# Row-tiled pairs for the last 64 rows of D, a 512-column gate|up operand, a new ScalarE order and an even spread of gradient pieces

## Chip, cores, metric

One core of a Trainium2 chip. The metric is device microseconds (us) of one execution, median of several. Before: 1578.2 us (1576.9 to 1579.3, 4 runs).

## The reference

The kernel gives the output and seven gradients of a gated mix: a = a 2-D FFT filter of x, b = a GEGLU feed-forward of x; out = g a + (1 - g) b with g = sigmoid(sum of x * gate_w).

```python
B, S, D, F = 1, 2048, 576, 4608
g = _sigmoid((x * gate_w).sum(-1, keepdims=True))
a = _A_ref(x, A_w_r, A_w_i)              # irfft2(rfft2(x) * W)
b = (_gelu(x @ w_gate) * (x @ w_up)) @ w_down
return g * a + (1 - g) * b               # and its vjp for grad_out
```

D = 576 is four and a half times 128. That half is what the change is about.

## The kernel before

First stage: 18 groups of 256 hidden columns x 8 steps of two 128-row tiles of x, 144 "hidden steps". A step computes gate and up of x and dOT (the gradient times w_down transposed), then GELU and its derivative. PSUM is the memory that TensorE writes its results to, in banks; ScalarE or VectorE must copy a result out before its bank can be used again. Into the steps are mixed "transform units" of the FFT (two PSUM banks, one unit at a time; a step has two places for them, its "half steps") and "gradient pieces" of the weights (dwd, dw, tail; two PSUM banks). A second stage reads the hidden gradients back and makes the outputs.

```python
DCH = [(0, 128), (128, 128), (256, 128), (384, 128), (448, 128)]  # last chunk overlaps, half zeroed
ph = ...tile_pool(name="ph", bufs=4, space=PSUM)   # 4 x one bank: gate, up, dOT of a step and one more
pw = ...tile_pool(name="pw", bufs=2, space=PSUM)   # gradient pieces
pf = ...tile_pool(name="pf", bufs=1, space=PSUM)   # transform units, two banks

def H_mm(g, tp):                                   # line 312
    for w, xt in ((wg_g, xT), (wu_g, xT), (wdT_g, dOT)):
        pt = ph.tile([P, TPB, FG], F32, tag="hps", name="hps")
        for tt in range(TPB):
            for ci in range(5):
                nc.tensor.matmul(pt[:, tt, :], lhsT=xt[:, ci, tp * TPB + tt, :], rhs=w[:, ci, :],
                                 start=(ci == 0), stop=(ci == 4))
# (cut) ScalarE in H_ew1: q, xb (gate), hu (up), om, s (sigmoids), da (dOT)
for step ...:
    fft_until(want(step, 0)); pts = H_mm(g, tp)
    tiles = H_ew1(g, tp, pts); fft_until(want(step, 1)); H_ew2(g, tp, tiles)
    for _ in range(quota[tp]):                     # quota = [0, 1, 1, 1, 2, 1, 2, 1]
        if pend: pend.pop(0)()                     # gradient pieces of the last group
# (cut) second stage: six transposing loads, then wd_all (3 x 1.7 MB), then the last pieces
```

## Time and profile before

| | before |
|---|---|
| time | 1578.2 us |
| TensorE busy | 1510 us, 96% |
| waiting of TensorE, from its start distances | 81 us |
| of it in 0 to 150 us / 150 to 1150 / 1150 to 1250 | 42 / 27 / 12 |

TensorE's busy time overlaps from matmul to matmul. "Waiting" here is each start-to-start distance less the time the earlier matmul streams (columns / 2.4 + 2.5 ns, that is 109 for 256 columns and 123 for 288, the distances that the trace shows where nothing waits). A pair that starts together counts once. This is worked out from the trace's records. Where the clock is at half, as in parts of the start, the slower streaming is in it too. The busy time by stretch (columns: stretch, length, busy us and count of TensorE, weight loads, VectorE, ScalarE, GpSimd, granted clock, DMA share, GB/s), kernel before:

```profile
0.00:150.00 150.00, 118.21 (x1070) 98.40 (x1071) 97.90 (x284) 107.22 (x191) 8.49 (x25) 0.94 0.50 133
150.00:400.00 250.00, 242.17 (x2192) 207.99 (x2190) 153.09 (x419) 161.56 (x310) 0.00 (x0) 1.00 0.37 103
400.00:650.00 250.00, 241.97 (x2184) 208.21 (x2183) 202.74 (x526) 165.37 (x321) 0.00 (x0) 0.99 0.47 134
```

TensorE is nearly full from 150 us on.

### The profile page before, as it was taken

The page shows a single profiled execution, that of the slowest core. Times are in us where ns is not written, and L with a number is a line of the kernel's source. Part 1 is how long each engine was busy: PE and PEld are TensorE (multiplying, and loading weights), DVE is VectorE, ACT ScalarE, POOL GpSimd, SP SyncE. Part 2 cuts the span into 40 slices and gives each one's busy share as a digit, 9 for nine tenths or more (in the row PEclk, how much of TensorE's full clock was granted, in tenths as well). Part 3 has the DMA queues.
Part 4 walks back from the last instruction along what each step waited for, and adds up shares of the span by engine and source line. Part 5 has one row for each costly group of instructions (what it writes and reads, how often), then busy time and mean ns, then how long its engine had stood idle before and what let it go on. Part 6 is the DMA issues. An engine that isn't in the chain of part 4 may idle for free.

```text
span 1576.6 us, 33157 instructions
## 1 busy us (share of the span) xinstructions
PE 1510.1 (96%) x13310; PEld 1270.9 (81%) x13310; DVE 813.9 (52%) x2154; ACT 738.8 (47%) x1395; POOL 26.3 (2%) x58
## 2 busy tenths in 40 slices
PE   6798999999999999999999999999997999999998
PEld 4577888888788888888888888888876777777776
DVE  5775565666887877865555646667103212121210
ACT  6777665765766766665666656656000000000000
POOL 1000000000000000000000000000000000000000
PEclk8999999999999999999999999999999999999999
DMA  6632432334544544453424434364899978787873
GB/s 140 198 102 78 113 99 82 109 97 132 140 134 120 151 124 129 132 152 93 124 82 135 127 97 128 101 145 122 241 192 214 212 153 172 155 171 154 170 150 69
DMA packets 513435, 214.45 MB, mean 136 GB/s; under 512 B 318080, under 2 KB 506368, under 8 KB 513280
## 3 DMA queue, kind: packets, MB, share of 16 engines
q1 hardware_dynamic: 511648, 207.61, 54.5%
q0 software_dynamic: 1632, 4.72, 1.1%
q8 instruction: 104, 1.70, 0.5%
q14 instruction: 51, 0.42, 0.1%
HBM read 41.77 MB, written 94.71 MB: 87 GB/s over the span
## 4 chain that ended last, share of the span: by engine, by line
PE 62%; issue 23%; DVE 6%; ACT 6%; DMA 1%; POOL 1%; SPq 1%; POOLq 0%; DVEq 0%; ACTq 0%
PE hps L312 25%; PE wps L392 15%; PE wps L376 7%; PE pf L640 3%; PE acc L833 2%; PE wps L403 2%; PE pf L433 2%; PE acc L875 2%; ACT da L334 1%; ACT om L330 1%; ACT q L323 1%; DMA pin<-scr 1%; PE pf L624 1%; PE pf L626 1%; ACT xb L324 1%
## 5 line engine op out<-in xcount | busy, mean ns | idle before, releaser
L312 PEld LDWEIGHTS <-xT 128*128 128x128 bf16 x2880 | 286.0, 99 | 39.6
L875 PEld LDWEIGHTS <-pin 128*128 128x128 bf16 x2304 | 225.4, 98 | 58.3 <-DMA pin<-scr 1.6
L392 PEld LDWEIGHTS <-xn 128*128 128x128 bf16 x2304 | 223.9, 98 | 30.3 <-issue 3.6
L312 PE MATMUL hps<-wg_g,xT 128*128 128x256 bf16 x1440 | 186.5, 278 | 0.0
L312 PE MATMUL hps<-wu_g,xT 128*128 128x256 bf16 x1440 | 183.8, 275 | 0.0
L312 PE MATMUL hps<-wdT_g,dOT 128*128 128x256 bf16 x1440 | 180.8, 273 | 0.0
L325 DVE TENSOR_SCALAR s<-q 128x512 bf16<-128x512 bf16 x144 | 42.0, 291 | 254.0 <-ACT q L323 253.8
L312 PEld LDWEIGHTS <-dOT 128*128 128x128 bf16 x1440 | 141.0, 98 | 16.4
L833 PE MATMUL acc<-wd_all,pin 128*128 128x288 bf16 x1152 | 145.4, 288 | 8.1 <-DMA pin<-scr 6.6
L376 PE MATMUL wps<-dB,A 128*128 128x288 bf16 x1152 | 152.2, 286 | 0.0
L875 PE MATMUL acc<-wuT,pin 128*128 128x288 bf16 x1152 | 143.4, 286 | 1.3 <-DMA pin<-scr 1.3
L833 PEld LDWEIGHTS <-pin 128*128 128x128 bf16 x1152 | 113.2, 98 | 38.5 <-DMA pin<-scr 7.5
L875 PE MATMUL acc<-wgT,pin 128*128 128x288 bf16 x1152 | 143.4, 286 | 0.0
L376 PEld LDWEIGHTS <-A 128*128 128x128 bf16 x1152 | 112.7, 98 | 27.6
L392 PE MATMUL wps<-dHu,xn 128*128 128x256 bf16 x1152 | 131.7, 273 | 0.0
L392 PE MATMUL wps<-dHg,xn 128*128 128x256 bf16 x1152 | 131.5, 273 | 0.0
L323 ACT ACTIVATE q<-hps 128x512 bf16<-128x512 f32 x144 | 86.1, 598 | 94.9 <-PE hps L312 94.9
L885 ACT COPY f32t<-acc 128x576 f32<-128x576 f32 x16 | 10.2, 638 | 250.5 <-PE acc L875 250.5
L334 ACT ACTIVATE da<-hps,omg 128x256 bf16<-128x256 f32 x288 | 118.1, 460 | 0.0
L887 DVE SCALAR_TENSOR_TENSOR f32t<-gwf,dlog,f32t 128x576 f32<-128x576 f32 x16 | 13.1, 818 | 179.1 <-ACT f32t L885 179.1
L330 ACT ACTIVATE om<-s 128x512 bf16<-128x512 bf16 x144 | 91.0, 632 | 24.5 <-DVE s L326 23.9
L331 ACT ACTIVATE s<-s 128x512 bf16<-128x512 bf16 x144 | 90.7, 630 | 4.6
(164 smaller groups left out, 1760.9 us busy)
## 6 DMA issues: line engine op xcount, KB each, us to landing
scr<-A SPq DMA_DIRECT2D x144, 128.0 KB, 1.9
scr<-dHg SPq DMA_DIRECT2D x144, 128.0 KB, 1.9
scr<-dHu SPq DMA_DIRECT2D x144, 128.0 KB, 1.9
out_dram<-dw SPq DMA_DIRECT2D x72, 128.0 KB, 1.8
out_dram<-dwd SPq DMA_DIRECT2D x36, 144.0 KB, 2.0
wd_all<-in_B_w_down_dram SPq DMA_DIRECT2D x3, 1728.0 KB, 12.6
scr_p<-Vt SPq DMA_DIRECT2D x32, 144.5 KB, 2.3
Vp<-scr_p SPq DMA_DIRECT2D x16, 289.0 KB, 3.4
```

Of the source, the lines that this page charges most:

```text
L312: nc.tensor.matmul(pt[:, tt, :], lhsT=xt[:, ci, tp * TPB + tt, :], rhs=w[:, ci, :], start=(ci == 0), stop=(ci == 4))
L323: nc.scalar.activation(q[:], hg[:], ACT.Square)
L325: V.tensor_scalar(s[:], q[:], A_GELU, 1.0, op0=ALU.mult, op1=ALU.add)
L330: nc.scalar.activation(om[:], s[:], ACT.Sigmoid, scale=-2.0 * C_GELU)
L331: nc.scalar.activation(s[:], s[:], ACT.Sigmoid, scale=2.0 * C_GELU)
L334: nc.scalar.activation(da[:, tt, :], da_ps[:, tt, :], ACT.Copy, scale=omg32[:, t0 + tt:t0 + tt + 1])
L376: nc.tensor.matmul(wps[:, :288], lhsT=tl(0, t)[:, fch * P:(fch + 1) * P], rhs=dB[:, t, h * 288:(h + 1) * 288], start=(t == 0), stop=(t == ...
L392: nc.tensor.matmul(wps[:, cc, :], lhsT=xn[:, t, (c0 + cc) * P:(c0 + cc + 1) * P], rhs=tl(k, t), start=(t == 0), stop=(t == T - 1))
L403: nc.tensor.matmul(wps[r0:r0 + 64, 0, :], lhsT=xn[:, t, 512:576], rhs=tl(k, t), start=(t == 0), stop=(t == T - 1))
L640: nc.tensor.matmul(yps[:, h, :288], lhsT=Z[:, lc, c, :], rhs=tb.At[lc][:, c, h * 288:(h + 1) * 288], start=(n == 0), stop=(n == 5))
L833: nc.tensor.matmul(bps[:, h, :288], lhsT=At[:, r, :], rhs=wd_all[:, fc, h * 288:(h + 1) * 288], start=(fc == 0), stop=(fc == NFC - 1))
L875: nc.tensor.matmul(xps[:, h, :288], lhsT=src[:, r, :], rhs=wT[:, h * 288:(h + 1) * 288], start=(k == 1 and f0 + r == 0), stop=(k == 2 and ...
```

## The change

The intent: do the 64 rows left over of D as "row pairs", two 64-row matmuls side by side in the two halves of the array, one for each of two tiles of x; put gate and up side by side as one 512-column operand; order ScalarE's reads so that PSUM is freed early; spread the gradient pieces one per step, carrying one into the next group's first step; and give steps with a short piece more transform units.

```diff
-    ph = ps1.enter_context(tc.tile_pool(name="ph", bufs=4, space=PSUM))
+    ph = ps1.enter_context(tc.tile_pool(name="ph", bufs=1, space=PSUM))
+    pz = ps1.enter_context(tc.tile_pool(name="pz", bufs=1, space=PSUM))
     def H_mm(g, tp):
+        if tp % 2 == 0:                               # dOT, for two steps
+            zt[0] = pz.tile([P, 2, 2, FG], F32, tag="z", name="z")
+            for t in range(t0, t0 + 4):
+                for ci in range(4): nc.tensor.matmul(... dOT[:, ci, t, :], rhs=wdT[:, ci, :] ...)   # cut
+            for t in range(t0, t0 + 4):
+                r = (LO, HI)[t % 2]
+                nc.tensor.matmul(... lhsT=dOT[r, 4, t, :], rhs=wdT[r, 4, :] ...)                    # cut
+        xy = ph.tile([P, 2, 2 * FG], F32, tag="xy", name="xy")
+        for tt, r in enumerate((LO, HI)):
+            nc.tensor.matmul(xy[:, tt, :], lhsT=xT[r, 4, t0 + tt, :], rhs=wgu[r, 4, :], start=True, stop=False)
+        for tt in range(TPB):
+            for ci in range(4): nc.tensor.matmul(xy[:, tt, :], ... rhs=wgu[:, ci, :] ...)           # cut
     # ScalarE: da, q, xb, hu first; the sigmoids behind the transform unit's copy
+            H_sig(tiles)
+            if carry:
+                carry.pop()()
     # pieces: dwd+dwd+dwd+dwd, dw, dw, tail, dw, dw  ->  spread
+        return [ud[0], dw1[0], ud[1], ud[2], ud[3], dw1[1], u_tail] + dw2
     # pace of the transform units
+    PACE = [0, 1, 3, 4, 6, 7, 8, 10, 11]
     # loads at the start: eight dOT transposes instead of four ahead of each further x load
     load_dOT(0)
+    load_dOT(2)
     for k in range(1, 4):
         load_x(4 * k)
-        load_dOT(2 * k)
+        load_dOT(4 * k)
+        load_dOT(4 * k + 2)
-    for u in pend:
+    for u in carry + pend:
```

Cut besides: doubled copies of the last 64 rows of the weights and of x in both halves, x's transposes through the gate|up and the transform tile, a pair in the forward transform, and the last copies of the dw pieces on ScalarE.

More of the change, by code (lines that the diff above doesn't have):

```diff
@@ L37 @@
 IMM = bass.MemoryType
-def load_w_dchunks(nc, eng, dst, w, fsl):
-    eng.dma_start(dst[:, 0:4, :], w[0:512, fsl].rearrange("(c p) f -> p c f", p=P))
-    eng.dma_start(dst[:, 4, :], w[DCH[4][0]:D, fsl])
+LO, HI = slice(0, 64), slice(64, 128)
 class Unit:
@@ L66, in iotas @@
     G.iota(tb.dcol[:, 0:4], pattern=[[128, 4]], base=0, channel_multiplier=1, **kw)
-    G.iota(tb.dcol[:, 4:5], pattern=[[0, 1]], base=DCH[4][0], channel_multiplier=1, **kw)
+    for r in (LO, HI):
+        G.iota(tb.dcol[r, 4:5], pattern=[[0, 1]], base=512, channel_multiplier=1, **kw)
     tb.krow = res.tile([P, P], F32, name="krow")
@@ L211, in load_w @@
         fsl = slice(g * FG, (g + 1) * FG)
-        wg_g = wpool.tile([P, 5, FG], BF16, tag="wg_g", name="wg_g")
-        wu_g = wpool.tile([P, 5, FG], BF16, tag="wu_g", name="wu_g")
-        wdT_g = wpool.tile([P, 5, FG], BF16, tag="wdT_g", name="wdT_g")
-        load_w_dchunks(nc, LD, wg_g, B_w_gate, fsl)
-        load_w_dchunks(nc, LD, wu_g, B_w_up, fsl)
-        LD.dma_start_transpose(wdT_g[:, 0:4, :], B_w_down[fsl, 0:512])
-        LD.dma_start_transpose(wdT_g[:, 4:5, :], B_w_down[fsl, DCH[4][0]:D])
-        return wg_g, wu_g, wdT_g
+        wgu = wpool.tile([P, 5, 2 * FG], BF16, tag="wgu", name="wgu")
+        wdT = wpool.tile([P, 5, FG], BF16, tag="wdT", name="wdT")
+        for k, w in enumerate((B_w_gate, B_w_up)):
+            cols = slice(k * FG, (k + 1) * FG)
+            LD.dma_start(wgu[:, 0:4, cols], w[0:512, fsl].rearrange("(c p) f -> p c f", p=P))
+            for r in (LO, HI):
+                LD.dma_start(wgu[r, 4, cols], w[512:D, fsl])
+        LD.dma_start_transpose(wdT[:, 4:5, :], B_w_down[fsl, DCH[4][0]:D])
+        LD.dma_start_transpose(wdT[:, 0:4, :], B_w_down[fsl, 0:512])
+        LD.dma_start(wdT[LO, 4, :], wdT[HI, 4, :])
+        return wgu, wdT
     def load_dOT(t):
@@ L223, in load_dOT @@
         LD.dma_start_transpose(dOT[:, 4:5, t, :], do_v[:, t, DCH[4][0]:D])
-    nc.gpsimd.memset(xT[0:D4NEW, 4, :, :], 0.0)
+    nc.gpsimd.memset(gwT[LO, 4:5], 0.0)
     ident = res.tile([P, P], BF16, name="ident")
@@ L230 @@
         nc.gpsimd.dma_start(gwT[:, 0:4], gate_w[0:512].rearrange("(c p) -> p c", p=P))
-        nc.gpsimd.dma_start(gwT[:, 4:5], gate_w[DCH[4][0]:D].rearrange("(p o) -> p o", o=1))
+        nc.gpsimd.dma_start(gwT[HI, 4:5], gate_w[512:D].rearrange("(p o) -> p o", o=1))
     def load_x(t0):
@@ L237, in load_do @@
         LD.dma_start(dB[:, t0:t0 + 4, :], do_v[:, t0:t0 + 4, :])
+    do_flat = grad_out[0].rearrange("(p t) d -> p (t d)", t=T)
     def load_dOT(t0):
@@ L241, in load_dOT @@
             LD.dma_start_transpose(dOT[:, 0:4, t, :], do_v[:, t, 0:512])
-            LD.dma_start_transpose(dOT[:, 4:5, t, :], do_v[:, t, DCH[4][0]:D])
-        nc.gpsimd.memset(dOT[0:D4NEW, 4, t0:t0 + 2, :], 0.0)
+            c0 = t * D + (512 if t % 2 == 0 else DCH[4][0])
+            LD.dma_start_transpose(dOT[:, 4:5, t, :], do_flat[:, c0:c0 + P])
     load_x(0)
@@ L269, in x_chunk @@
     def x_chunk(t0, act):
-        for k, c0 in enumerate((0, 2, 4)):
-            nc_ = min(2, 5 - c0)
-            tp_ = ph.tile([P, 2, 4, P], BF16, tag="hps", name="tp")
-            for c in range(nc_):
-                d0 = DCH[c0 + c][0]
-                for tt in range(4):
-                    nc.tensor.transpose(tp_[:, c, tt, :], xn[:, t0 + tt, d0:d0 + 128], ident[:])
-            p0 = D4NEW if c0 == 4 else 0
-            o, i = xT[p0:, c0:c0 + nc_, t0:t0 + 4, :], tp_[p0:, 0:nc_]
+        tp_ = ph.tile([P, 2, 2, 4, P], BF16, tag="xy", name="tp")
+        tl_ = pf.tile([P, 2, 2, 4, P], BF16, tag="pf", name="tl")
+        for h in range(2):
+            for c in range(2):
+                d0 = DCH[2 * h + c][0]
+                for tt in range(4):
+                    nc.tensor.transpose(tp_[:, h, c, tt, :], xn[:, t0 + tt, d0:d0 + 128], ident[:])
+        for tt in range(4):
+            for r in (LO, HI):
+                nc.tensor.transpose(tl_[r, 0, 0, tt, :], xn[:, t0 + tt, 512:D], ident[:])
+        for k in range(3):
+            o = xT[:, 2 * k:2 * k + 2, t0:t0 + 4, :] if k < 2 else xT[:, 4, t0:t0 + 4, :]
+            i = tp_[:, k] if k < 2 else tl_[:, 0, 0]
             if k in act:
@@ L303 @@
     kept = {}
+    zt = [None]
     def H_mm(g, tp):
-        wg_g, wu_g, wdT_g = wts[g]
-        out = []
-        for w, xt in ((wg_g, xT), (wu_g, xT), (wdT_g, dOT)):
-            pt = ph.tile([P, TPB, FG], F32, tag="hps", name="hps")
-            for tt in range(TPB):
-                for ci in range(5):
-                    nc.tensor.matmul(pt[:, tt, :], lhsT=xt[:, ci, tp * TPB + tt, :], rhs=w[:, ci, :],
-                                     start=(ci == 0), stop=(ci == 4))
-            out.append(pt)
-        return out
+        wgu, wdT = wts[g]
+        t0 = tp * TPB
+        if tp % 2 == 0:
+            zt[0] = pz.tile([P, 2, 2, FG], F32, tag="z", name="z")
+            for t in range(t0, t0 + 4):
+                for ci in range(4):
+                    nc.tensor.matmul(zt[0][:, t % 2, (t - t0) // 2, :], lhsT=dOT[:, ci, t, :], rhs=wdT[:, ci, :],
+                                     start=(t < t0 + 2 and ci == 0), stop=False)
+            for t in range(t0, t0 + 4):
+                r = (LO, HI)[t % 2]
+                nc.tensor.matmul(zt[0][:, t % 2, (t - t0) // 2, :], lhsT=dOT[r, 4, t, :], rhs=wdT[r, 4, :],
+                                 start=False, stop=t >= t0 + 2)
+        xy = ph.tile([P, 2, 2 * FG], F32, tag="xy", name="xy")
+        for tt, r in enumerate((LO, HI)):
+            nc.tensor.matmul(xy[:, tt, :], lhsT=xT[r, 4, t0 + tt, :], rhs=wgu[r, 4, :], start=True, stop=False)
+        for tt in range(TPB):
+            for ci in range(4):
+                nc.tensor.matmul(xy[:, tt, :], lhsT=xT[:, ci, t0 + tt, :], rhs=wgu[:, ci, :], start=False, stop=(ci == 3))
+        return xy[:, :, 0:FG], xy[:, :, FG:2 * FG], zt[0][:, :, tp % 2, :]
     def H_ew1(g, tp, pts):
@@ L322, in H_ew1 @@
         xb, q, s, om, hu, da = (ewt(n) for n in ("xb", "q", "s", "om", "hu", "da"))
-        nc.scalar.activation(q[:], hg[:], ACT.Square)
-        nc.scalar.copy(xb[:], hg[:])
+        t0 = tp * TPB
+        for tt in range(TPB):
+            nc.scalar.activation(da[:, tt, :], da_ps[:, tt, :], ACT.Copy, scale=omg32[:, t0 + tt:t0 + tt + 1])
+        nc.scalar.activation(q[:], hg, ACT.Square)
+        nc.scalar.copy(xb[:], hg)
+        nc.scalar.copy(hu[:], hu_ps)
         V.tensor_scalar(s[:], q[:], A_GELU, 1.0, op0=ALU.mult, op1=ALU.add)
@@ L328, in H_ew1, with H_sig @@
         V.tensor_tensor(q[:], xb[:], q[:], op=ALU.mult)
-        nc.scalar.copy(hu[:], hu_ps[:])
+        return xb, q, s, om, hu, da
+    def H_sig(tiles):
+        xb, q, s, om, hu, da = tiles
         nc.scalar.activation(om[:], s[:], ACT.Sigmoid, scale=-2.0 * C_GELU)
         nc.scalar.activation(s[:], s[:], ACT.Sigmoid, scale=2.0 * C_GELU)
-        t0 = tp * TPB
-        for tt in range(TPB):
-            nc.scalar.activation(da[:, tt, :], da_ps[:, tt, :], ACT.Copy, scale=omg32[:, t0 + tt:t0 + tt + 1])
-        return xb, q, s, om, hu, da
     def H_ew2(g, tp, tiles):
@@ L388, in f @@
             def f():
+                late = k == 2 and c0 + TPB >= 4
                 wps = pw.tile([P, TPB, FG], F32, tag="wps", name="wps")
@@ L394, in f @@
                 dw = stage.tile([P, TPB, FG], BF16, tag="dw", name="dw")
-                wevac(dw[:], wps[:])
+                (nc.scalar.copy if late else wevac)(dw[:], wps[:])
                 LD.dma_start(ov[:, c0:c0 + TPB, fsl], dw[:])
@@ L408, in u_tail @@
             LD.dma_start(out_5[512:576, fsl], dw[64:128, :])
-        us = [u_dw(1, o4v, c0) for c0 in range(0, 4, TPB)]
+        dw1, dw2 = ([u_dw(k, ov, c0) for c0 in range(0, 4, TPB)] for k, ov in ((1, o4v), (2, o5v)))
         ud = [u_dwd(fch, h) for fch in range(FCH) for h in range(2)]
-        us = us + ud if g == 0 else ud + us
-        us += [u_tail]
-        us += [u_dw(2, o5v, c0) for c0 in range(0, 4, TPB)]
-        return us
+        if g == 0:
+            return dw1 + ud + [u_tail] + dw2
+        return [ud[0], dw1[0], ud[1], ud[2], ud[3], dw1[1], u_tail] + dw2
     side = []
@@ L431, in f @@
                 for c in range(2):
-                    for ci in range(5):
+                    for ci in range(4):
                         nc.tensor.matmul(yps[:, c, :DF], lhsT=src[:, ci, t, :], rhs=tb.Dt[ci][:, c, :],
-                                         start=(ci == 0), stop=(ci == 4))
+                                         start=(ci == 0), stop=False)
+                for c in range(2):
+                    r = (LO, HI)[c if src is xT else t % 2]
+                    nc.tensor.matmul(yps[:, c, :DF], lhsT=src[r, 4, t, :], rhs=tb.Dt[4][r, c, :], start=False, stop=True)
                 ys[t] = unit([2, DF], name="Y")
@@ L463, in f @@
             for c in range(2):
-                for ci, (d0, dn) in enumerate(DCH):
-                    nc.tensor.transpose(tps[:, c, d0:d0 + dn], tb.Dt[ci][:, c, l0:l0 + ln], ident[:])
+                for ci in range(4):
+                    nc.tensor.transpose(tps[:, c, ci * P:(ci + 1) * P], tb.Dt[ci][:, c, l0:l0 + ln], ident[:])
+                nc.tensor.transpose(tps[:, c, 512:D], tb.Dt[4][LO, c, l0:l0 + ln], ident[LO, LO])
             o = unit([2, D], name="At")
@@ L676 @@
     LAST = NG * NT - 16
+    PACE = [0, 1, 3, 4, 6, 7, 8, 10, 11]
+    slot0 = 2 * NT - 4
     done = [0]
@@ L684, in want @@
         else:
-            n = 2 * NT - 4 + (n_slots - 2 * NT + 4) * (h - 2 * NT) / (2.0 * (LAST - NT))
+            tp = step % NT
+            n = slot0 + (n_slots - slot0) * ((step - tp - NT) / NT + (PACE[tp] + half * (PACE[tp + 1] - PACE[tp]) / 2) / PACE[NT]) \
+                / ((LAST - NT) / NT)
         return int(min(n, n_slots) + 1e-9)
@@ L705, in f @@
             gate(4 * k)
-            if k < 3:
-                load_dOT(4 + 4 * k)
-                load_dOT(6 + 4 * k)
             if k == 3:
@@ L732 @@
     pend = []
-    quota = [0, 1, 1, 1, 2, 1, 2, 1]
+    carry = []
+    quota = [0, 1, 1, 1, 2, 1, 1, 1]
     for g in range(NG):
@@ L756 @@
                     side.pop(0)()
-        assert not pend
+        assert len(pend) <= 1
+        carry = pend
         pend = W_units(g)
```

## The prediction

> **What bounds the kernel now.** I read the page first (busy shares and costliest groups), then busy time by stretch, then the order of time of one steady stretch, then the waits, then the SP queue's first microseconds. The page's first part and its TensorE rows:
>
> ```profile
> PE 1510.1 (96%) x13310; PEld 1270.9 (81%) x13310; DVE 813.9 (52%) x2154; ACT 738.8 (47%) x1395; POOL 26.3 (2%) x58
> ...
> L312 PE MATMUL hps<-wg_g,xT 128*128 128x256 bf16 x1440 | 186.5, 278 | 0.0
> L312 PE MATMUL hps<-wu_g,xT 128*128 128x256 bf16 x1440 | 183.8, 275 | 0.0
> L312 PE MATMUL hps<-wdT_g,dOT 128*128 128x256 bf16 x1440 | 180.8, 273 | 0.0
> ```
>
> A busy TensorE alone proves nothing, since matmuls overlap. So I read starts in the order of time:
>
> ```profile
> 376.62 1.25 PE L312 MATMUL hps<-wg_g,xT 128*128 128x256 bf16 x10
> 377.71 1.25 PE L312 MATMUL hps<-wu_g,xT 128*128 128x256 bf16 x10
> 378.81 1.25 PE L312 MATMUL hps<-wdT_g,dOT 128*128 128x256 bf16 x10
> 379.90 0.29 PE L516 MATMUL pf<-Vp,Btab 128*128 128x289 bf16 x1
> ...
> 380.27 0.29 PE L519 MATMUL pf<-Vp,Btab 128*128 128x289 bf16 x1
> 380.49 0.30 PE L403 MATMUL wps<-dHg,xn 128*64 128x256 bf16 x1
> 380.49 0.30 PE L403 MATMUL wps<-dHu,xn 128*64 128x256 bf16 x1
> 380.62 0.27 PE L403 MATMUL wps<-dHg,xn 128*64 128x256 bf16 x1
> ...
> 382.15 0.27 PE L403 MATMUL wps<-dHu,xn 128*64 128x256 bf16 x1
> 382.36 3.67 PE L392 MATMUL wps<-dHu,xn 128*128 128x256 bf16 x32
> 385.86 0.29 PE L516 MATMUL pf<-Vp,Btab 128*128 128x289 bf16 x1
> ```
>
> Ten 256-column matmuls start within 1.09 us, so one costs 0.109 us and its weight load is hidden. A step's 30 of them (line 312) take 3.28 us and everything else in the step follows without a gap. I subtracted from each start-to-start distance in the trace the streaming time of the earlier matmul (columns at 2.4 per ns plus 2.5 ns); what is left is waiting. It sums to 81 us of 1576.6: 42 before 150 us, 27 between 150 and 1150 us, 12 between 1150 and 1250 us. TensorE streaming therefore is the bound from 150 us on; in the first 150 us it is a chain of loads, transposes and PSUM copies. The other engines have room in the steady part:
>
> ```profile
> 150.00:1110.00 960.00, 941.55 (x8560) 813.40 (x8558) 636.63 (x1705) 608.80 (x1169) 0.00 (x0) 1.00 0.43 119
> ```
>
> (TensorE, weight loads, VectorE 66%, ScalarE 63%.)
>
> **What the Trainium skill says.** "TensorE: Matmul & The Clock Gate", section "Back-to-back issue gap", gives N/2.4 + 2.5 ns at the warm clock; for 256 columns 109.2 ns, which this trace shows. The same page, section "Part 3: Packing small matmuls", says that tiles in different row groups run together, about 4 ns apart. The kernel before has no row pair, but its column pair (line 403) starts together and advances every 0.109 us, so a pair costs one matmul. "TensorEngine Tiling (Array Packing)", section "Key Properties", says that changing the tiling mode drains the TensorE. The trace agrees: into the column pair the start comes 217 ns after a matmul that streams 123 (94 extra), and the first pair lasts 130 instead of 109 (21 extra); out of it 205 instead of 109 (96 extra) and 10 more on the next. A round trip costs about 0.22 us. "PSUM — Partial Sum Buffer", section "The four PSUM rules", holds one matmul's output to one bank, 512 fp32 values; the code fits this (a 512-column tile per bank), and it is why double buffering is lost below.
>
> **The change part by part.**
>
> *Removed in line 312's work.* The fifth D chunk was zero-padded 64 rows to 128, so it cost a full matmul. Per step now: gate and up together, two row tiles x 4 matmuls of 512 columns plus one row pair of 512. By N/2.4 + 2.5, a 512-column one is 215.8 ns (an estimate; no such matmul is in this trace), so 9 x 215.8 = 1.942 us against 20 x 109.2 = 2.184. For dOT, per two steps: 16 full matmuls and two pairs, 18 x 109.2 = 1.966 against 20 x 109.2, so 0.983 per step against 1.092. Sum: 2.925 instead of 3.276 us, 0.351 saved per step, x 144 steps = **-50.5 us**, if pairs overlap fully.
>
> *Removed in the forward transform.* Ten 289-column matmuls become eight and a pair: one of 0.123 us saved, x 32 = **-3.9 us**.
>
> *Added: mode changes.* In an even step the order is full dOT matmuls, dOT pairs, xT pair, full xT: one round trip. In an odd step the xT pair comes first: again one. 144 x 0.22 = **+31.7 us**. Transform units: 32 pairs, of which 9 stand directly ahead of an odd step's xT pair by my count of the schedule and share its switch; 23 x 0.22 = **+5.1 us**. I assume that row tiling drains as long as the column tiling measured here. This is the largest uncertain term: the drains eat two thirds of the gain.
>
> *Start.* The SP queue issues transposes one by one:
>
> ```profile
> 9.00 1.26 SPq L241 DMA_TRANSPOSE dOT<-in_grad_out_dram  x1
> 10.31 1.23 SPq L242 DMA_TRANSPOSE dOT<-in_grad_out_dram  x1
> 11.59 0.58 SPq L234 DMA_DIRECT2D xn<-in_A_x_dram  x1
> 12.21 1.22 SPq L241 DMA_TRANSPOSE dOT<-in_grad_out_dram  x1
> ```
>
> Now eight of them instead of four stand ahead of the second x load (and of the third and fourth): 4 x 1.25 = 5 us, plus the copy of the doubled wdT rows, which must wait for its transpose. The first step multiplies dOT first and needs t = 0 to 3, landed at about 22 us, where the first matmul now starts at 9.5; and the transposes of x share the one gate|up PSUM tile. I get steps 1 to 3 some 10 us later (gate|up of step 1 at 33 to 34 us against 22.9). Later loads are then already done, and some of the 42 us of early waiting can absorb it: **+8 us**.
>
> *PSUM.* Four one-bank tiles become one two-bank gate|up tile and one two-bank dOT tile for two steps. The next gate|up may start only when ScalarE has read the last: 0.598 + 0.582 + 0.589 = 1.77 us, with latency about 2.2 us. Between two gate|up blocks stand a gradient piece (1.96 us for 16 x 0.1225; 1.87 for the tail; 3.5 for 32 x 0.109) and one or two transform units, and in even steps dOT's 2 us. It nearly always covers 2.2 us, and putting the dOT scaling first and the sigmoids last keeps ScalarE free. About zero.
>
> *Spreading.* The carried piece removes the gaps where two transform units met with nothing between. One such gap now:
>
> ```profile
> 397.27 0.29 PE L519 MATMUL pf<-Vp,Btab 128*128 128x289 bf16 x1
> 399.09 0.28 PE L516 MATMUL pf<-Vp,Btab 128*128 128x289 bf16 x1 [1.53 <-ACT Xx L524]
> ```
>
> Counting the schedule, 8 such meetings after step 9 fall away (1.7 us each in the trace: 14), but the new pacing puts 15 doubles into single half steps, 8 ahead of the step's matmuls (about 0.9 us: latency and a 0.65 us copy) and 7 behind them (about 2.2, as the copy queues behind the three reads): 22 us. Shorter pieces that fail to cover a copy cost a few us less than now. **+3 us**.
>
> *Second stage.* Nothing changes but that one more gradient piece lies ahead of it, so its first loads have 3.5 us longer: of the 12 us waiting there **-2 us**.
>
> Sum: -50.5 - 3.9 + 31.7 + 5.1 + 8 + 3 - 2 = -8.6 us, from 1578.6 to about 1570. Since ScalarE's new order and the even spread were chosen for this kernel and my count of doubles takes the worst for each, I lean 4 us lower: 1566.
>
> **Rivals.** (1) *Row drains are cheap.* Weight loads for another row group may overlap, and then the change brings up to -54 us less 10 to 15: 1535 to 1545. For it: within the column pair the second load costs only 3 ns. Against: the way out of column mode, into ordinary full matmuls, costs 96 ns too, so it is the array that empties, not the kind of load. (2) *The single gate|up buffer becomes the bound.* Where ScalarE waits for VectorE ahead of a sigmoid, the next reads come late and TensorE stands. Between 400 and 650 us VectorE is busy 203 of 250 us, so it can happen there; 0.3 us per step over all 144 would cost 43 us, giving about 1610. Against: the gate reads now stand ahead of the sigmoids, and ScalarE has a third of its time free. (3) *The start decides.* If none of its 10 us is absorbed and the clock drops in the new gaps (it was 0.69 between 20 and 30 us), it is +12 to +15: about 1574.
>
> **Range and chances.** The drain term moves by half its size at most in my view (15 us either way), the waits by 15, the start by 6; together about 20 us either side: 1540 to 1590. Faster by over 2% means under 1547: it needs rival 1, or drains a third cheaper together with fewer waits; 0.2. Slower by over 2% means over 1610, rival 2 in full: 0.04. Within 2%: 0.76.
>
> **What would show it.** Right: 512-column matmuls 0.216 us apart; row pairs starting within 5 ns of each other; about 95 to 115 ns extra at each change of mode; TensorE streaming with drains about 18 us less than now; gate|up of step 1 at about 33 us; waits on the transform's PSUM tile at doubled units. Wrong: extra at a change of mode well under 60 or over 150 ns; pairs that start one after the other; long waits ahead of the gate|up pair on ScalarE's hu copy; a second stage that moves by more than 5 us.

## The result, and the profile after

1614.4 us (1612.1 to 1619.4, 4 runs): **slower, ratio 1.0234** (95% interval 1.0209 to 1.0260). A ratio is the mean time of one kernel's fast runs over that of the other's in the same rounds, so it is not quite the ratio of the medians. I had 1566, a range of 1540 to 1590, and a chance of 0.04 for slower by over 2%.

I lined up the two traces by the start of each odd step's gate matmul, us:

| start of step | before | changed, later by | e2, later by | e10, later by |
|---|---|---|---|---|
| 1 | 22.9 | 8.6 | 8.6 | 4.3 |
| 9 | 87.9 | 20.0 | 20.4 | 15.0 |
| 47 | 386.4 | 23.0 | 16.9 | 8.9 |
| 57 | 456.8 | 38.6 | 20.2 | 10.6 |
| 79 | 622.5 | 25.7 | 5.8 | -3.8 |
| 143 | 1099.6 | 21.4 | -8.0 | -17.6 |
| end of the span | 1576.6 | 33.8 | 6.5 | -10.0 |

(e2 and e10 are experiments below.) So the changed kernel lost 20 us by step 9, 1.4 us more in the 134 steps that follow, where the gain should have come, and 12.4 us more behind the loop, 3.5 of which are only the carried piece that now runs there. (Two profiles of one and the same kernel, e6 and e10, differ by 1 us at step 9.)

Split by start distances, steps 9 to 143 have these parts, in us:

| steps 9 to 143 | before | changed | e2 |
|---|---|---|---|
| streaming | 981 | 929 | 929 |
| changes of mode | 3 | 34 | 33 |
| waits | 27 | 50 | 21 |

The last row has the slower streaming at half clock in it, about 2, 8 and 4 us. The intended saving is there (3.5 of the 52 us of streaming is the carried piece), and so are the mode changes; the waits took the rest.

TensorE's rows on the page of the changed kernel:

```profile
PE 1493.4 (93%) x11755; PEld 1083.6 (67%) x11886; DVE 805.1 (50%) x2148; ACT 740.1 (46%) x1401; POOL 22.5 (1%) x51
...
L336 PE MATMUL xy<-wgu,xT 128*128 128x512 bf16 x1021 | 258.0, 386 | 16.1 <-issue 13.5
```

There is less to do, and more time. (1021 of the 1152 full gate|up matmuls have a record; most of those missing stand just behind a pair. I counted 0.216 us for each, so sums of waiting are good to a few us; e2's trace, which has them all, streams the same 929 us.) An even step of the changed kernel in the order of time:

```profile
298.66 1.91 PE L325 MATMUL z<-wdT,dOT 128*128 128x256 bf16 x16
300.50 0.39 PE L329 MATMUL z<-wdT,dOT 64*128 64x256 bf16 x4
300.73 0.38 PE L333 MATMUL xy<-wgu,xT 64*128 64x512 bf16 x2
301.04 1.90 PE L336 MATMUL xy<-wgu,xT 128*128 128x512 bf16 x7
302.78 3.66 PE L418 MATMUL wps<-dHu,xn 128*128 128x256 bf16 x32
```

This part is as intended. The two matmuls of a gate|up pair start 3 ns apart (median), full 512-column ones follow each other in 216 ns. The way into row mode costs 96 ns beyond streaming (median of 169) and the way out about the same (96 ns in the traces that hold the first full matmul). The z and xy pairs share one stay in row mode.

What is not as intended stands in three places. First, the start (TensorE before, with the first and the second step's gate; then queue and TensorE, changed kernel):

```profile
9.51 2.29 PE L312 MATMUL hps<-wg_g,xT 128*128 128x256 bf16 x10
...
22.91 2.29 PE L312 MATMUL hps<-wg_g,xT 128*128 128x256 bf16 x10
```

```profile
18.18 1.23 SPq L247 DMA_TRANSPOSE dOT<-in_grad_out_dram  x1
19.46 0.58 SPq L236 DMA_DIRECT2D xn<-in_A_x_dram  x1
...
19.62 1.03 PE L325 MATMUL z<-wdT,dOT 128*128 128x256 bf16 x4 [1.57 <-DMA dOT<-in_grad_out_dram]
...
20.98 0.64 PE L333 MATMUL xy<-wgu,xT 64*128 64x512 bf16 x2
...
26.80 1.05 PE L283 MATMUL tp<-ident,xn 128*128 128x128 bf16 x16 [1.65 <-ACT hu L350]
...
31.52 0.61 PE L333 MATMUL xy<-wgu,xT 64*128 64x512 bf16 x2
```

The brackets give TensorE's idle time and what ended it: the fourth transpose pair of dOT holds the first gate|up until 21 us, and x's transposes for the next step then wait for the gate|up tile to be read.

Second, transform units that meet, and a load that comes late (TensorE and ScalarE, changed kernel):

```profile
224.45 0.29 PE L478 MATMUL pf<-Y,Rt 128*128 128x289 bf16 x1
224.77 0.58 ACT L349 CAST xb<-xy 128x512 bf16<-128x512 f32 x1
225.24 0.60 ACT L350 CAST hu<-xy 128x512 bf16<-128x512 f32 x1
225.71 0.67 ACT L480 CAST Vt<-pf 128x578 bf16<-128x578 f32 x1
226.44 0.28 PE L475 MATMUL pf<-Y,Rt 128*128 128x289 bf16 x1 [1.70 <-ACT Vt L480]
...
417.41 0.42 PE L545 MATMUL pf<-Vp,Btab 128*128 128x289 bf16 x1 [5.78 <-DMA Vp<-scr_x]
```

The second unit of a half step needs the transform tile, whose copy stands behind gate|up's three reads. And at 417 us TensorE had stood since 411.6 us for a unit whose input's load the queue issued only at 414.3 us. Two more long waits are for the copy out of the transform tile (TensorE and ScalarE, changed kernel):

```profile
183.09 2.09 PE L458 MATMUL pf<-Dt,xT 128*128 128x289 bf16 x8 [5.72 <-ACT Vt L480]
...
454.10 0.64 ACT L617 CAST Vt<-pf 128x578 bf16<-128x578 f32 x1 [3.58 <-DMA scr_p<-Vt]
```

At 183 us ScalarE had spent 175.8 to 180.3 us on a table of the transform before it came to da, the three reads and the copy; at 455 us the copy itself had waited 3.6 us for the store of an earlier unit.

Third, the passage to the second stage (changed kernel, all engines):

```profile
1142.43 7.08 SPq L825 DMA_DIRECT2D wd_all<-in_B_w_down_dram  x3
1149.61 5.04 SPq L422 DMA_DIRECT2D out_dram<-dw  x2
...
1160.46 0.58 ACT L387 CAST dw<-wps 128x512 bf16<-128x512 f32 x1 [20.40 <-DMA out_dram<-dw]
...
1161.10 9.26 PE L418 MATMUL wps<-dHu,xn 128*128 128x256 bf16 x64 [14.15 <-ACT dw L387]
```

Read it upwards: TensorE waits 14 us for a PSUM copy, that copy waits for a staging tile, and that tile for a store that queued behind 5 MB of loads. Before, the same queue stood there, and a copy waited as long (ScalarE, kernel before):

```profile
1138.36 0.58 ACT L362 CAST dw<-wps 128x512 bf16<-128x512 f32 x1 [14.69 <-DMA out_dram<-dw]
```

But then two of the last four dw pieces were staged and the other two fitted into the two PSUM banks, so TensorE went on. Now a carried dw piece holds one of the two staging tiles as well, its store behind the same loads.

### The profile page after: what moved, and what is told of

Read it like the earlier page. It is cut to its first block, busy times and chain, and to the rows that moved or that the text cites. A ratio compares the mean times of both kernels' runs of the same rounds, so it can differ in the third digit from the quotient of the medians.

```text
span 1610.4 us, 30114 instructions
## 1 busy us (share of the span) xinstructions
PE 1493.4 (93%) x11755; PEld 1083.6 (67%) x11886; DVE 805.1 (50%) x2148; ACT 740.1 (46%) x1401; POOL 22.5 (1%) x51
## 4 chain that ended last, share of the span: by engine, by line
PE 78%; issue 10%; ACT 4%; DVE 3%; SPq 2%; DMA 2%; POOL 0%; POOLq 0%; DVEq 0%; ACTq 0%
PE wps L418 15%; PE xy L336 15%; PE acc L910 11%; PE wps L401 8%; PE z L325 8%; PE acc L868 7%; PE pf L669 3%; PE xy L333 2%; PE wps L429 2%; PE pf L458 2%; PE z L329 1%; ACT xb L349 1%; PE pf L653 1%; DMA out_dram<-dw 1%; PE pf L655 1%
## 5 line engine op out<-in xcount | busy, mean ns | idle before, releaser
L336 PE MATMUL xy<-wgu,xT 128*128 128x512 bf16 x1021 | 258.0, 386 | 16.1 <-issue 13.5
L418 PEld LDWEIGHTS <-xn 128*128 128x128 bf16 x2304 | 227.7, 99 | 51.6 <-issue 14.8
L336 PEld LDWEIGHTS <-xT 128*128 128x128 bf16 x1152 | 102.1, 99 | 146.7 <-issue 47.4
L347 ACT ACTIVATE da<-z,omg 128x256 bf16<-128x256 f32 x288 | 120.9, 473 | 105.0 <-PE z L329 105.0
L348 ACT ACTIVATE q<-xy 128x512 bf16<-128x512 f32 x144 | 86.0, 597 | 148.5 <-PE xy L336 148.5
L325 PE MATMUL z<-wdT,dOT 128*128 128x256 bf16 x1152 | 144.7, 281 | 6.9 <-DMA dOT<-in_grad_out_dram 6.9
L325 PEld LDWEIGHTS <-dOT 128*128 128x128 bf16 x1152 | 114.4, 100 | 26.3 <-DMA dOT<-in_grad_out_dram 8.4
L920 ACT COPY f32t<-acc 128x576 f32<-128x576 f32 x16 | 10.2, 638 | 250.3 <-PE acc L910 250.3
L367 DVE TENSOR_TENSOR om<-om,q 128x512 bf16<-128x512 bf16 x144 | 61.2, 425 | 75.6 <-ACT om L359 68.3
```

The source lines that it names most:

```text
L325: nc.tensor.matmul(zt[0][:, t % 2, (t - t0) // 2, :], lhsT=dOT[:, ci, t, :], rhs=wdT[:, ci, :], start=(t < t0 + 2 and ci == 0), stop=False)
L336: nc.tensor.matmul(xy[:, tt, :], lhsT=xT[:, ci, t0 + tt, :], rhs=wgu[:, ci, :], start=False, stop=(ci == 3))
L347: nc.scalar.activation(da[:, tt, :], da_ps[:, tt, :], ACT.Copy, scale=omg32[:, t0 + tt:t0 + tt + 1])
L348: nc.scalar.activation(q[:], hg, ACT.Square)
L367: V.tensor_tensor(om[:], om[:], q[:], op=ALU.mult)
L418: nc.tensor.matmul(wps[:, cc, :], lhsT=xn[:, t, (c0 + cc) * P:(c0 + cc + 1) * P], rhs=tl(k, t), start=(t == 0), stop=(t == T - 1))
```

## The experiments

All twelve gave the reference's result. The kernels of a call (e1 to e4; e5 to e8; e9 to e11; e12) ran on one chip, beside the kernel before; each call had another set of runs of the kernel before, so kernels are compared by ratios. A 95% interval of the difference of two ratios, worked out from theirs, is 5 to 6 us either way. Where a step below rests on less, the line-up of the traces has to carry it.

**e1: the start.**

```diff
-    load_dOT(0); load_dOT(2);  x loads with two load_dOT each
+    load_dOT(0);  x loads with one load_dOT each, the rest in the first steps (as before)
+    first = g == 0 and tp == 0        # in the first step: gate|up, then dOT; da behind hu
```

> Changed kernel (1614 us), with the loads of dOT back in the order of the kernel before and, in the first step alone, gate|up ahead of dOT and ScalarE's dOT scaling last. Theory: the start lost 20 us by step 9 (line-up of the two traces), about 8 of it because the first gate|up waits for the dOT transposes of t = 0 to 3; this edit gives back 5 to 8 us, so about 1607. Rival (the start is lost to the one shared PSUM tile that x's transposes and gate|up take turns in): under 3 us, 1612 to 1615.

Measured 1609.5 us, ratio 1.0197: 0.0037 x 1578 = 5.8 us less than the changed kernel. Step 1 starts 5.3 us later than before instead of 8.6, step 9 14.8 instead of 20.0. The two edits, the order of the loads and that of the first step, were made together and are a quarter of the start's loss, as expected; the larger part is something else.

**e2: the pace.**

```diff
-            n = slot0 + (n_slots - slot0) * (... PACE[tp] + half * (PACE[tp + 1] - PACE[tp]) / 2 ...)
+            n = slot0 + (n_slots - slot0) * (h - 2 * NT) / (2.0 * (LAST - NT))
```

> Changed kernel with the even pacing of the transform units of the kernel before; pieces and carry stay as changed. Theory: the uneven pacing puts two units into one half step 15 times, which costs about 20 us of waits on the transform's single PSUM tile, and brought the 5.8 us wait for a load at 417 us; even pacing gives back 10 to 20 us: 1594 to 1604. Rival (the waits come from late PSUM reads on ScalarE whatever the pacing): within 4 us of 1614.

Measured 1581.6 us, ratio 1.0022: **33 us less**, well over what I expected. The line-up (table above) is the same as the changed kernel's up to step 9 and then wins steadily. Busy time by stretch, changed kernel, then e2:

```profile
150.00:400.00 250.00, 237.16 (x1825) 162.60 (x1855) 147.27 (x412) 163.90 (x313) 0.00 (x0) 0.99 0.35 101
400.00:650.00 250.00, 233.01 (x1808) 162.82 (x1840) 194.78 (x510) 160.90 (x316) 0.00 (x0) 0.98 0.45 130
```

```profile
150.00:400.00 250.00, 246.42 (x1899) 166.41 (x1899) 149.63 (x418) 165.24 (x314) 0.00 (x0) 0.99 0.36 103
400.00:650.00 250.00, 247.60 (x1951) 172.31 (x1950) 207.96 (x543) 170.73 (x336) 0.00 (x0) 0.99 0.47 137
```

TensorE gets 9 and 15 us fuller, and in e2 hardly a wait over 0.3 us is left between 200 and 1100 us but one of 2.6 us at 411. In the changed kernel 14 meetings of two units there cost 18 us together (0.9, 1.5 or 1.9 us each; I had estimated 22 for 15). What I had not counted are three long waits: 5.9 us at 417 (2.6 in e2), 3.6 us at 455 (gone), 5.9 us at 183 us (3.4). With them it is 27 of the 33 us (29.8 in the two traces between steps 9 and 143). Some 4 more are clock: after long waits the changed kernel's trace has the clock at half for 20.4 us between 110 and 1110 us, e2's for 10.2, and the distances of the matmuls there come out 7.9 and 4.2 us longer.

**e3: the large loads behind the pieces.**

```diff
+    for u in carry + pend:
+        u()
     for f0 in range(0, NFC, FCB):
         LD.dma_start(wd_all[...], ...)
-    for u in carry + pend:
-        u()
```

> Changed kernel, but the three large loads of wd_all are issued after the last gradient pieces instead of ahead of them. Theory: the 14.2 us stop of TensorE at 1147 to 1161 us is a gradient piece's store that queues behind those loads, while only two staging tiles exist; with the loads behind, the stop is gone: 8 to 13 us less, 1601 to 1606. Rival (the stop is only moved, since the second stage then waits for wd_all): within 3 us of 1614.

Measured 1605.7 us, ratio 1.0172: 9.8 us less. The stop of 14 us is gone; shorter waits of 2 to 4 us for loads appear later, so part of it did move. In the line-up the stretch behind the loop loses 7.0 us instead of 12.4.

**e4: the pairs undone.**

```diff
-            for r in (LO, HI):
-                LD.dma_start(wgu[r, 4, cols], w[512:D, fsl])
+            LD.dma_start(wgu[HI, 4, cols], w[512:D, fsl])
+        nc.gpsimd.memset(wgu[LO, 4, :], 0.0)      # and the same for wdT; dOT's last rows all in HI
-            nc.tensor.matmul(xy[:, tt, :], lhsT=xT[r, 4, t0 + tt, :], rhs=wgu[r, 4, :], ...)
+            nc.tensor.matmul(xy[:, tt, :], lhsT=xT[:, 4, t0 + tt, :], rhs=wgu[:, 4, :], ...)
```

> Changed kernel with the row pairs of the hidden steps undone: the last 64 rows of D as full 128-row matmuls with a zeroed half, same order, same 512-column operand, same PSUM. Theory: a step loses the pairs' gain (0.216 + 0.109 = 0.325 us) and regains one round trip of mode changes (0.22 us measured): 0.10 us a step, 15 us slower over 144 steps: about 1629. Rival (the mode changes cost more than the pairs bring, they are the reason for the slower time): 1614 or faster.

Measured 1630.0 us, ratio 1.0325: 14.4 us slower than the changed kernel, and 14.3 us slower in the line-up between steps 9 and 143. (The edit also drops the loads and the copy that double the rows; that belongs to the pairs.) The pairs are worth what the sum said, 0.325 us gained less 0.22 us of mode changes in each step. They are not the reason for the slower time.

**e5: e1, e2 and e3 together.**

> The edits of e1 (start), e2 (even pacing) and e3 (large loads behind the last pieces) together on the changed kernel. Alone they gave back about 5, 33 and 9 us. Theory (three separate losses, in three stretches of the run): they add, 47 us less than 1614, about 1567. Rival (they share one cause, late PSUM reads on ScalarE, so that the largest of them takes the others with it): 1575 to 1582.

Measured 1573.2 us, ratio 0.9955 (0.9929 to 0.9981). From the changed kernel that is 44 us by the ratios, between the two theories and nearer to the sum, which the noise does not exclude. In the line-up the start gives 4.4 of its 5 us and the pace its 30; behind the loop 8.6 us are lost instead of 12.4, where e3 alone lost 7.0.

**e6: two more edits.**

```diff
-        tp_ = ph.tile([P, 2, 2, 4, P], BF16, tag="xy", name="tp")
+        tp_ = [pw.tile([P, 2, 4, P], BF16, tag="wps", name="tp") for _ in range(2)]
+        # forward transform of dOT: last rows as a full matmul, Dt[4] with one half zeroed
```

> e5 with two more edits: x's transposes use the two gradient PSUM banks, idle in the first steps, instead of the gate|up tile; and the transform of dOT takes its last 64 rows as a full matmul with a zeroed half, since both of its halves stand in the same row group there and never ran side by side. Theory: steps 1 to 3 no longer wait about 2 us each for ScalarE's hu read ahead of x's transposes, 5 us; 16 round trips of mode change fall away, 3 us: about 8 us below e5, 1559. Rival (the start is held by the loads alone): within 4 us of e5.

Measured 1567.7 us, ratio 0.9926: 4.6 us below e5, not 8. Step 9 stands 16.0 us behind, e5's 15.6: **taking x's transposes out of the gate|up tile gave nothing that shows**, so that half of the theory fell: their waits on hu (2.1 us in e5's trace) are gone, and others grew. (The edit also puts 1.7 us of copies and fills on VectorE at 15 us.) The 4 us came later, between steps 23 and 57: 2.5 by step 47, in the stretch where the dOT transform runs (229 to 373 us in the changed kernel), and 1.5 after it, which the theory doesn't cover. The dOT transform's "pairs" had both matmuls in the same row group and started 134 ns apart, one after the other (in 11 of the 16 units, by the changed kernel's trace; others had a record between): they paid the mode change and saved nothing. I had missed this in the diff. (4.6 us is within the noise of the times; the traces of e10 and e12, with the same edit, also gain 4.2 us on e5's between steps 23 and 57.)

**e7: the spread alone, on the kernel before.**

```diff
-        us = us + ud if g == 0 else ud + us
+        return [ud[0], dw1[0], ud[1], ud[2], ud[3], dw1[1], u_tail] + dw2   # carry, quota as changed
```

> The kernel before with only the even spread of the gradient pieces (new order, one piece carried into the next group's first step, its last pieces ahead of the large loads); no row pairs, old PSUM layout, old even pacing of the transform units. Theory: the spread is good in itself, it removes most of the 27 us of waits between 150 and 1150 us that stand where no piece lies between two transform units: 8 to 15 us below before, 1563 to 1570. Rival (the waits merely move): within 4 us of 1578.

Measured 1581.3 us, ratio 1.0008: the theory fell. The meetings in the first step of a group are gone, but behind a lone dwd piece waits of 2.3 to 3.4 us appeared (at 465 and 584 us the longest), since in the old ScalarE order the transform's copy comes after the sigmoids and dOT's scaling. The edit also put the large loads late, and waits in 1110 to 1300 us rose from 12 to 17 us, so the total is not a clean test of the spread; the line-up is. Steps 9 to 143 take 4.2 us less, 3.5 of them the carried piece, and their waits sum to 27 us as before: the rival holds.

**e8: the gate|up pair last.**

```diff
-        (xT pair), then (full xT matmuls)
+        (full xT matmuls), then (xT pair)
```

> e5 with the gate|up row pair behind its full matmuls instead of ahead of them. Then an even step has two stretches of row mode instead of one, and a transform unit's pair ahead of an odd step no longer shares the change: 72 + 9 more round trips. Theory (a round trip costs TensorE about 0.2 us wherever it stands): 16 us slower than e5. Rival (a mode change is hidden when a long matmul follows, so the order does not matter): within 4 us of e5.

Measured 1588.0 us, ratio 1.0052, against e5's 0.9955: 15.3 us slower for 81 more round trips, 0.19 us each. The trace counts 547 changes of mode for 387, again 80 round trips. "Pairs first" is worth that.

**e9: the old ScalarE order, in the new layout.**

```diff
+        sigmoids, then da, in H_ew1 (ahead of the second half's transform units)
-            H_sig(tiles)
```

> e5 (1573 us) with ScalarE's order of the kernel before: sigmoids and the dOT scaling of a step ahead of the transform unit's PSUM copy, so that this copy comes some 2 us later. The spread alone on the kernel before brought nothing: waits of 2.4 to 3.4 us appeared behind short pieces. Theory: the spread needs the new order, because a 1.96 us piece covers the copy only when it stands ahead of the sigmoids; with the old order 8 to 20 us come back: 1581 to 1593. Rival (the order is worth nothing, the even pacing and the edits to start and end did it all): within 4 us of e5.

Measured 1653.6 us, ratio 1.0464: **80 us slower than e5**, four times the upper end. TensorE's longest waits in e9:

```profile
PE z L323 <- ACT da L360: 22.9, 21, 2.5
PE pf L459 <- ACT Vt L481: 20.6, 14, 3.7
```

(us in all, times, longest.) With one dOT tile for two steps, the next dOT matmuls wait for da; with one transform tile, the next unit waits for a copy behind sigmoids. Between steps 9 and 143 the waits sum to 96 us, 20 in e5. The kernel before has this order with four gate|up|dOT tiles and 27 us of waits there; the new order was not tried in that layout.

**e11: the old order of pieces, in the new layout.**

```diff
-        return [ud[0], dw1[0], ud[1], ud[2], ud[3], dw1[1], u_tail] + dw2
+        us = us + ud if g == 0 else ud + us            # then tail, then dw's second half
-    quota = [0, 1, 1, 1, 2, 1, 1, 1]                   # and the carried piece
+    quota = [0, 1, 1, 1, 2, 1, 2, 1]
```

> e5 (1573 us) with the gradient pieces in the order and share per step of the kernel before, nothing carried. Theory: in each group's first step two transform units meet again without a piece between them; about 12 such meetings at about 1 us, since the copy is now early: 8 to 14 us slower, 1581 to 1587. Rival (with the new ScalarE order no spread is needed): within 4 us of e5.

Measured 1600.5 us, ratio 1.0135: 28 us slower than e5, twice what I expected. TensorE's waits in e11:

```profile
PE pf L467 <- ACT Vt L489: 16.1, 7, 5.4
...
PE xy L334 <- ACT hu L355: 10.9, 10, 1.7
```

The same lines for e5:

```profile
PE pf L466 <- ACT Vt L488: 12.3, 6, 4.7
...
PE xy L334 <- ACT hu L355: 2.0, 2, 1.5
```

Of the 28 us by step 143, 3.5 are the piece that isn't carried out of the loop, and 24 are waits (44 us against 20). The second line has grown most: a group's first step has no piece, and gate|up of the next step waits for ScalarE's read of the last. It is the price of the single gate|up tile, which the carried piece hides. The rest is spread over many waits.

**e10 and e12: the best version.** e10 is e6 once more with five rounds.

> The kernel of e6 once more, with more rounds, as the best version found: 0.99 to 0.995 of the kernel before, about 1567 us. Theory: start 16 us slower than before, second stage about as before, steady steps about 30 us faster over the whole. Rival (the lead of e6 was that chip's): 1.0.

Measured 1568.5 us, ratio **0.9935 (0.9922 to 0.9947)**: it beats both kernels, the one before by 0.65%: clear of noise, but small. Its start is 15 us behind, steps 9 to 143 are 33 us faster (3.5 of which moved behind the loop).

e12 is e6 with gate|up ahead of dOT in the whole first group.

```diff
-        first = g == 0 and tp == 0
+        first = g == 0
```

> e10 with gate|up ahead of dOT, and the dOT scaling behind the three reads of gate|up, in all eight steps of the first group instead of the first step alone. Open is why the start of e10 is still 16 us behind the kernel before at step 9. Theory: the first steps are a chain of latencies, and with dOT ahead ScalarE gets its first input only at the end of a step's matmuls; with gate|up ahead, its 1.77 us of reads run beside dOT's 2 us in four steps: 4 to 8 us less, 1561 to 1565. Rival (the start is held by ScalarE's and VectorE's own work, tables and copies): within 2 us of e10, 1568.

Measured 1569.1 us, ratio 0.9947 (0.9930 to 0.9964), step 9 17.3 us behind: the theory fell. Waits up to step 9 are some 2 us less than in e10, but more of the start ran at half clock, which costs 4 us more there. So this order brings no time as it stands; that it is worth nothing at an equal clock isn't shown.

## Why the prediction was wrong

The time lies above the range, in the case that I gave 0.04. I had tied that case to rival 2; it came without it (TensorE waited 0.4 us for a read of gate|up between 107 and 1110 us). Term by term:

| term as predicted | predicted | measured |
|---|---|---|
| row pairs of the hidden steps, less mode changes (-46.8 + 31.7) | -15 | -14.4 (e4) |
| 512 columns instead of 256 (the rest of -50.5) | -4 | 216 ns each, as estimated |
| forward transform (-3.9 + 5.1) | +1 | not measured apart; the dOT half saves nothing |
| start | +8 | +20.0 (step 9) |
| spreading and pacing | +3 | about +22: waits from step 9 to 143 are 27 us before, 50 changed (21 in e2) |
| second stage | -2 | +8.9 (12.4 less the carried piece); e3 takes 9.8 away by the times, 5.4 by the traces |

The bound and the largest term were **right**: TensorE streaming bounds the steps, row tiling drains like column tiling (96 ns each way), a pair costs one matmul. Rival 1 (cheap drains) is out.

**"Spreading: +3 us" failed most.** My count of meetings was nearly right (15 counted, 14 found, 18 us instead of 22). But I netted it against 14 us of waits removed, and with the even pace (e2) only 6 are removed in all (27 to 21): the meetings go, and other waits come. And I took the rest of the schedule as unchanged. The uneven pace put units where their input's load was not yet issued (417 us), where ScalarE made a table first (183 us) and where a store still held the copy's target (455 us): three waits of 4 to 6 us, 15 together. I had priced two units that meet, and not what else a unit waits for.

**"Second stage: -2 us" had the wrong sign.** I reasoned that one more piece ahead of it gives its loads more time. My own sign of being wrong, over 5 us there, came true. The trace before already showed a copy that waited 14.7 us for a staging tile behind those loads. One more dw piece used up the slack and TensorE stopped.

**"Start: +8 us" was half of it or less.** Step 1 came at 31.5 us (I said 33 to 34), so the loads were read rightly. But I expected the early waits to absorb the delay; instead it grew from 8.6 us at step 1 to 20.0 at step 9. The loads' order and the first step's order explain 5 us (e1). Undoing the shared gate|up tile of x's transposes (e6) and dOT ahead of gate|up (e12) brought nothing. What the remaining 15 us consist of can be worked out from e10's start distances up to step 9 (half clock where the clock record says so, and before its first entry, where 128-column transposes start 0.107 us apart instead of 0.056): streaming 43 us (47 before), slower streaming at half clock 15 (9), changes of mode about 5 (none), waits about 36 (27). So the clock is some 6 us of it, the changes of mode 5, waits 9, less 4 of streaming. Of the waits, 4.8 us are for dOT's loads (none before); why the others grew, and why the clock is lower, stays open.

"PSUM: about zero" held, but only with the rest of the change: without the new ScalarE order (e9) or without the spread (e11) the same layout costs 80 or 28 us more than e5. I had argued these from latencies; without either, the layout is slower than the kernel before. Rival 2, the single gate|up buffer, is real in e11 and hidden in the changed kernel.

## What to carry to other kernels

A change that saves 0.1 us in each step of a saturated engine can be lost in a few places outside the steady step: line up two traces by step number first, and look where the lag jumps. When a buffer count goes to one, the order of the reader's queue and what stands between two uses decide; test them in the new layout, since on the old one they may seem worthless, as the spread did (e7). Row pairs pay only where two matmuls in different row groups share a stay in row mode: weigh what a pair saves against 0.2 us per round trip.

## What the Trainium skill lacked or had wrong

- "TensorEngine Tiling (Array Packing)", section "Key Properties", says that a change of mode drains the TensorE but gives no time. Here: 96 ns into row mode and about 96 ns out of it beyond streaming; e8's 81 added round trips cost 15.3 us, 0.19 us each. So by this sum (neither was run alone) a lone 256-column pair, 0.109 us saved, loses and a 512-column one, 0.216, is about even.
- "TensorE: Matmul & The Clock Gate", section "Back-to-back issue gap", gives about 131 ns per matmul for N = 512 in a stream with weight loads and says N/2.4 + 2.5 over-counts there. Here 512-column matmuls, each with its weight load, started 216 ns apart (median of 877 distances in the changed kernel, none under 200 ns): the formula is right and the 131 ns were not seen.
